# Seven-product Up from the middle of the second chunk on, instead of from the third chunk on

## The chip, the core and the metric

The kernel runs on one core of one Trainium2 chip. The metric is the device time of one execution in microseconds. In the profile the engines are PE (TensorE, the matmul engine; PEld is its weight load), DVE (VectorE), ACT (ScalarE), POOL (GpSimd) and SP (SyncE, which issues most of the DMAs).

## What is computed

An mLSTM cell over 4 batches, 8 heads, 768 steps and a head dimension of 40, followed by a feed-forward block. Cut to what matters, the reference is:

```python
# cell, for every step t:  C and n are the state, m a running maximum
m_new = max(f + m, i);  fs = exp(f + m - m_new);  is_ = exp(i - m_new)
C = fs * C + is_ * outer(v, k);   n = fs * n + is_ * k
y = sigmoid(o) * (C @ q) / max(abs(n @ q), 1)
# feed-forward on x = y, as (3072 tokens, 320)
h = x @ w_in            # 320 -> 2048
g = h * cos(h)
out = g @ w_out         # 2048 -> 320
```

## The kernel before

The sequence is cut into 6 chunks of 128 steps (C = 128, B = 4 batches, NC = 6). A cell is one chunk of one batch: n = chunk * 4 + batch, N = 24. The cell is computed in chunk form: scores (L553), a weighing by decays (`decay_exponents` on POOL, `decay` on ACT, `weigh` on DVE), values (L568) that also read the carried state, and the increment of the state (`seam`, `state`, `fade`).

The feed-forward part of chunk c runs while the cells of chunk c + 1 are computed. It has 16 blocks of 128 hidden units; a **slot** (c, f2), f2 = 0 to 7, takes two of them: Up (x @ w_in for 512 tokens and two blocks), the gate (near, rest, sin, gate), and a share of the down products. A cell takes two slots: slots 2b and 2b + 1 hold cell n = (c + 1) * 4 + b.

The order of work on each engine is the order of the program: everything runs under `tc.manual_schedule()`, so an instruction that waits holds up all that stands behind it on its engine. Between engines there are only the waits that data asks for.

There are two kinds of Up:

- `Up` (L731): per slot four 128x512 matmuls (L749) and two for the last 64 dimensions (L743). It is used in chunks 0 and 1.
- `UpFast` (L806): the same 2x2 block product with seven half-size products (L817, 256 columns) instead of eight. It reads sums of the weights (S1, S2, S4 and, in place of A21, S3, made by `up_weight_sums` on POOL, L779) and sums of x (T1, T2, T4 and one block of x changed in place, made by `x_sums` on POOL, L798 to L804). Its first product is S2 by T2, its second S3 by the changed block of x. After four products ACT copies both banks out (L825, L826), `fill()` puts down products on TensorE in between, three products follow, POOL adds up the copies (L834 to L836), and `join` (L839) adds them on DVE to what stands in PSUM. Gate 0 is then a DVE instruction (L769), gate 1 one of POOL (L852). It is used from chunk `fast` = 2 on.

The two orders of a slot are written out by hand: `both_parts` (for `Up`) and `both_parts_fast` (for `UpFast`), and the main loop chooses between them by chunk. In `both_parts_fast` the scores of a cell are made one slot ahead, so its first slot has an order of its own (`first`).

The down products are taken from a generator, `products_of(c)`: 96 per chunk, 12 for each slot's pair of blocks; `down_slot` (L1068) says how many run in a slot, `fill_in` how many lie between the products of an Up. In chunk 1 seven slots run 12 each, and the last 12 run in slot (2,0) and (2,1). In later chunks slots 2 to 7 run 14 each.

Further names in what follows: `turn_blocks` (L532) transposes q and k of a cell on DVE (L538); `scale_q` (L540) multiplies the turned q by the carried decay on POOL (L542) into qG; `weight_sums(part)` (L883) makes the sums for the down products on POOL, two pairs of blocks per part (L891 to L894); `weigh_k` is L481, `odd_values` L487, `fade` L684, `state` L726; `sums` (L896) is L902 to L905. L1014 is the matmul of a down product. Each float32 matmul shows as two records in the trace.

In `both_parts`, the end of the second slot of a cell is, before the change:

```python
turn_blocks(n + 1)
if n + 1 < (fast + 1) * B:
    scale_q(n + 1)
if b > 0:
    up_weight_sums(b - 1)
if b == B - 1:
    x_sums(c + 1)
```

Of the kernel before, what the change touches and what calls it, by code (L numbers as in the profile page):

```python
# [29 lines left out]
def kernel(  # L30
# [22 lines left out]
    B, H, S, D = q.shape  # L53
# [546 lines left out]
    def normalize_turned(n):  # L600
        denominators(n)
        divide(n)
# [169 lines left out]
    wi = w_in_sb.rearrange("p i (f e n) -> p i f e n", e=2, n=128)  # L772
    A11, A12, A21, A22 = (wi[:, i, :, e] for e in range(2) for i in range(NK))
    HB = B // 2 * C
    fast = 2
    Sw, Tx = {}, {}
    x_room = const.tile([128, 3 * B // 2, C], FP, name="x_room")

    def up_weight_sums(part):  # L779

        tt = nc.gpsimd.tensor_tensor
        S1, S2, S4 = (room[:, i] for i in range(3))
        Sw[0] = S1, S2, S4, A21
        if part == 0:
            tt(out=S1, in0=A21, in1=A22, op=OP.add)
            tt(out=S2, in0=S1, in1=A11, op=OP.subtract)
        elif part == 1:
            tt(out=S4, in0=A12, in1=S2, op=OP.subtract)
        r = ((), range(0, 4), range(4, NF // 2))[part]
        if r:  # L790
            r = slice(r[0], r[-1] + 1)
            tt(out=A21[:, r], in0=A11[:, r], in1=A21[:, r], op=OP.subtract)

    def x_block(c, i, t):
# [259 lines left out]

    def filled(c, f2):

        return c >= fast

    def products_of(c):
        if c not in made_of:  # L1060
# [7 lines left out]
    def down_slot(c, f2):  # L1068

        if c == 0:  # L1070
            if f2 > 0:
                down(0, f2 - 1)
            return
        if f2 == 0:
            if c == 1:
                down(0, LAST)
            else:
                run(made_of[c - 1], 12 - 2 * FILL)
            return
        if f2 == 1 and c > 1:  # L1080
            run(late_products(c - 1), NF)
            return
        each = 14 if c == NC - 1 else 12
        quota = [0] * 8
        for m in range(2, 8):
            quota[m] = each * 7 * (m - 1) // 6 - each * 7 * (m - 2) // 6
        if c == NC - 1:
            quota = [0, 0, 14, 14, 14, 14, 14, 21]
        run(products_of(c), each if c == 1 else quota[f2] - FILL * filled(c, f2))

    pw, pmu = (ps_u.tile([128, HP, C], FP, name=name, tag="up") for name in ("pw", "pmu"))

# [354 lines left out]
    def both_parts(c, b):  # L1447

        n = (c + 1) * B + b
        for i in range(2):  # L1450
            f2 = 2 * b + i
            up = Up(c, f2)
            if i == 0:
                scores(n)
            elif n % 2 == 1 and n + 3 < N:
                load_two(n + 3)
            for e in range(2):
                up.near(e)
            for e in range(2):
                up.rest(e)  # L1460
            if i == 0:
                weigh(n)
                decay_exponents(n + 1)
                for e in range(2):
                    up.sin(e)
                    up.gate(e)
                sums(c, f2)
                if b == B - 1:
                    sigmoid_in_place(c + 2)
                decay(n + 1)  # L1470
            else:
                seam_out(n)
                state(n)
                for e in range(2):
                    up.sin(e)
                    up.gate(e)
                sums(c, f2)
                weigh_k(n + 1)
                odd_values(n + 1)
            down_slot(c, f2)  # L1480
            if i == 0:
                values(n)
                seam(n)
                normalize_turned(n)
                fade(n)
                if b < 3:
                    weight_sums(b + 1)
                load_blocks(n + 2)
                load_E(n + 3)
                if b == B - 2:  # L1490
                    load_o(c + 2)
                sin_next()
            else:
                turn_blocks(n + 1)
                if n + 1 < (fast + 1) * B:
                    scale_q(n + 1)
                if b > 0:
                    up_weight_sums(b - 1)
                if b == B - 1:
                    x_sums(c + 1)  # L1500

    def both_parts_fast(c, b):

        n = (c + 1) * B + b
        cell, follows = n < N, n + 1 < N
        first = (c, b) == (fast, 0)
        ahead = {0: 3, B - 1: 2}.get(b, H - 2)
        pool = nc.gpsimd if cell else nc.vector
        for i in range(2):
            f2 = 2 * b + i  # L1510
            up = UpFast(c, f2, lambda: fill_in(c, f2))
            if f2 == 0:
                if cell:
                    place_gates(c + 1)
                if cell and not first:
                    weigh_k(n)
                sin_next()
            if f2 == 2 * B - 2 and c + 2 < NC:
                sigmoid_in_place(c + 2)
                sin_next()  # L1520
            if cell and i == 0:
                if first:
                    scores(n)
                    scale_q(n)
                else:
                    values(n)
                    seam(n)
                    if f2 > 0 and follows:
                        turn_blocks(n + 1)
                if follows:  # L1530
                    decay_exponents(n + 1)
            if cell and i == 1:
                if follows:
                    decay(n + 1, range(ahead, H))
                    sin_next()
                    if f2 > 1:
                        scores(n + 1)
                if n % 2 == 1 and n + 3 < N:
                    load_two(n + 3)
                if b == B - 1:  # L1540
                    x_sums(c + 1)
                    if follows:
                        scale_q(n + 1)
                elif follows:
                    weigh_k(n + 1)
                    odd_values(n + 1)
                    scale_q(n + 1)
                if b == 0:
                    if first:
                        fade(n)  # L1550
                    sums(c, 0, pool)
            up.join()
            if first and i == 0:
                weigh(n)
            for e in range(2):
                up.near(e)
            for e in range(2):
                up.rest(e)
            if f2 == 2 and cell:
                combine_late(c - 1)  # L1560
            if cell and i == 0 and not first:
                fade(n)
            if cell and i == 1:
                seam_out(n)
            for e in range(2):
                up.sin(e)
                up.gate(e)
            if f2 == 0 and follows:
                turn_blocks(n + 1)
            if f2 == 1 and cell:  # L1570
                state(n)
            if f2 == 0 and not cell:
                sums(c, 0, pool)
            if f2 == 2:
                sums(c, 1, pool)
            down_slot(c, f2)
            if f2 == 1 and follows:
                scores(n + 1)
            if f2 == 0:
                for p in range(2):  # L1580
                    combine_first(c - 1, p)
                for p in range(2):
                    combine_x(c - 1, p)
            if cell and i == 0:
                if follows:
                    decay(n + 1, range(ahead))
                if first:
                    values(n)
                    seam(n)
                normalize_turned(n)  # L1590
                if n + 2 < N:
                    load_blocks(n + 2)
                if n + 3 < N:
                    load_E(n + 3)
                if b == B - 2 and c + 2 < NC:
                    load_o(c + 2)
            if i == 0:
                if f2 > 0:
                    if cell:
                        state(n)  # L1600
                    sums(c, f2)
            if i == 1:
                if follows:
                    if b == B - 1:
                        odd_values(n + 1)
                    weigh(n + 1)
                if b == 0:
                    combine_y(c - 1)
                    if not cell:
                        combine_late(c - 1)  # L1610
                else:
                    sums(c, f2)

    pieces, outs = [], []
    with tc.manual_schedule():
        first_cells()
        first_period()
        for b in range(1, B):
            first_parts(b)
        for c in range(1, NC):  # L1620
            for b in range(B):
                (both_parts_fast if c >= fast else both_parts)(c, b)
        run(made_of[NC - 1], 21)
        combine_last()

# [29 lines left out]
```

## Time and profile before

| | |
|---|---|
| median of 3 runs | 505.82 us (504.16 to 506.86) |
| the profiled execution | 503.72 us, span 501.9 us |
| granted TensorE clock over the span | 1.00 |
| busy: PE, DVE, ACT, POOL | 495.1, 420.6, 332.5, 300.0 us |
| slots (1,4) to (1,7), starts | 154.18, 165.25, 173.11, 184.18 us |
| slots (2,0) to (2,2), starts | 192.04, 202.15, 213.07 us |

Busy times are unions of the instructions of an engine. The starts are those of the first matmul of each Up in the timeline of TensorE; the length of a slot is the distance to the next start. A group in brackets, [5.55 <-DVE t L538], is idle time of that engine ahead of the instruction, and what ended it.

### The profile page before, as it was taken

The numbers are of one execution on the slowest core, as the hardware profiler recorded it, in microseconds if no ns is written. First come the engines' busy times: TensorE is split into PE (matmuls) and PEld (weight loads), VectorE is DVE, ScalarE is ACT, GpSimd is POOL, SyncE is SP. The second block draws the span as 40 slices with busy tenths as digits, with TensorE's granted clock in tenths as the row PEclk, the third lists the DMA queues.
The fourth block names the chain that finished last, engine by engine and source line by source line (L and its number), as shares of the span: only waits on it lengthen the run. The fifth ranks groups of instructions, "written<-read, shape, count | busy, mean of one in ns | idle before, by whom it ended". The sixth has DMA issues, their size and how long they took to land.

```text
span 501.9 us, 11143 instructions
## 1 busy us (share of the span) xinstructions
PE 495.1 (99%) x4038; PEld 375.4 (75%) x4038; DVE 420.6 (84%) x842; ACT 332.5 (66%) x646; POOL 300.0 (60%) x394
## 2 busy tenths in 40 slices
PE   9999999999999999999999999999999999999997
PEld 6856656565667668887887888788788888787876
DVE  7899998999878878899889889889979866777565
ACT  6799997878564575765877846777847743443541
POOL 8254557666555576787558877657567446434340
PEclk9999999999999999999999999999999999999999
DMA  9989899997366346129446118628113000010001
GB/s 139 182 223 239 213 224 279 233 217 136 114 178 111 101 120 127 50 86 202 132 125 106 48 54 195 168 83 150 43 35 85 1 7 5 2 54 0 2 0 54
DMA packets 100663, 56.74 MB, mean 113 GB/s; under 512 B 63456, under 2 KB 93360, under 8 KB 100608
## 3 DMA queue, kind: packets, MB, share of 16 engines
q1 hardware_dynamic: 97408, 54.43, 46.8%
q10 hardware_dynamic: 2896, 1.23, 1.0%
q8 instruction: 32, 0.52, 0.5%
q0 software_dynamic: 304, 0.36, 0.3%
q14 instruction: 23, 0.19, 0.1%
HBM read 50.66 MB, written 4.10 MB: 109 GB/s over the span
## 4 chain that ended last, share of the span: by engine, by line
PE 85%; ACT 4%; DVE 3%; DMA 2%; SPq 2%; POOL 2%; issue 1%; DVEq 0%; ACTq 0%; POOLq 0%
PE acc L1014 24%; PE pup L817 17%; PE pup L749 9%; PE po L863 6%; PE pup L833 6%; PE late L1014 5%; PE ps L560 4%; PE pup L743 3%; PE vt L595 2%; PE vt L586 2%; PE pu L701 2%; PE ph L576 1%; DMA E<-M_d 1%; DMA vs<-in_v_dram 1%; DVE n L760 1%
## 5 line engine op out<-in xcount | busy, mean ns | idle before, releaser
L757 ACT ACTIVATE n<-pup 128x512 int32<-128x512 f32 x64 | 37.0, 593 | 84.2 <-DVE pup L842 58.4
L765 ACT ACTIVATE n<-n 128x512 f32<-128x512 f32 x96 | 57.7, 626 | 16.5 <-DVE n L760 12.5
L852 POOL TENSOR_TENSOR g<-g,n 128x512 f32<-128x512 f32 x31 | 39.6, 1278 | 47.5 <-ACT n L765 47.4
L749 PE MATMUL pup<-xT,w_in_sb 128*128 128x512 f32 x128 | 58.7, 601 | 0.3 <-ACT xT L712 0.2
L1014 PE MATMUL acc<-w_out_sb,g 128*128 128x160 f32 x320 | 58.7, 303 | 0.0
L760 DVE SCALAR_TENSOR_TENSOR n<-pup,n 128x512 f32<-128x512 f32 x64 | 43.1, 689 | 18.5 <-ACT n L757 15.9
L834 POOL TENSOR_TENSOR blocks<-blocks 128x256 f32<-128x256 f32 x32 | 25.1, 785 | 54.5 <-ACT blocks L826 54.5
L1014 PE MATMUL acc<-T,g 128*128 128x160 f32 x304 | 56.4, 301 | 0.0
L817 PE MATMUL pup<-xT,w_in_sb 128*128 128x256 f32 x192 | 53.5, 385 | 0.2
L476 ACT ACTIVATE E<-E,tab 128x128 f32<-128x128 f32 x160 | 50.1, 389 | 4.3 <-POOL E L462 4.1
L1014 PEld LDWEIGHTS acc<-w_out_sb,g 128*128 128x128 f32 x320 | 49.0, 190 | 4.7 <-issue 2.7
L769 DVE TENSOR_TENSOR g<-pup,n 128x512 f32<-128x512 f32 x64 | 42.7, 687 | 5.7 <-ACT n L765 4.8
L1014 PEld LDWEIGHTS acc<-T,g 128*128 128x128 f32 x304 | 46.5, 190 | 1.1 <-issue 0.4
L749 PEld LDWEIGHTS pup<-xT,w_in_sb 128*128 128x128 f32 x128 | 23.1, 189 | 30.7 <-issue 30.0
L825 ACT COPY blocks<-pup 128x512 f32<-128x512 f32 x32 | 18.6, 582 | 34.2 <-PE pup L817 33.8
L817 PEld LDWEIGHTS pup<-xT,w_in_sb 128*128 128x128 f32 x192 | 33.8, 189 | 9.6 <-ACT blocks L826 4.4
L817 PE MATMUL pup<-x_room,room 128*128 128x256 f32 x128 | 38.5, 382 | 0.0
L542 POOL TENSOR_TENSOR qG<-t,G 128x512 f32<-128x512 f32 x20 | 26.4, 1321 | 16.7 <-DVE t L538 16.7
L1014 PE MATMUL acc<-T,blocks 128*128 128x160 f32 x160 | 36.2, 308 | 0.2 <-POOL blocks L904 0.2
L863 PE MATMUL po<-w_out_sb,g 128*128 128x320 f32 x128 | 36.2, 436 | 0.1
L833 PE MATMUL pup<-xL,w_in_l 64*128 64x512 f32 x128 | 36.1, 641 | 0.0
L566 DVE TENSOR_TENSOR E<-ps,E 128x512 f32<-128x512 f32 x46 | 29.5, 682 | 5.8 <-PE ps L560 5.6
(227 smaller groups left out, 1210.7 us busy)
## 6 DMA issues: line engine op xcount, KB each, us to landing
E<-M_d SPq DMA_DIRECT2D x20, 512.0 KB, 6.0
qr<-in_q_dram SPq DMA_DIRECT2D x72, 80.0 KB, 2.6
kr<-in_k_dram SPq DMA_DIRECT2D x72, 80.0 KB, 2.2
bits<-in_moe_w_out_dram SPq DMA_DIRECT2D x8, 640.0 KB, 6.2
G<-G_d SPq DMA_DIRECT2D x18, 256.0 KB, 5.7
blocks<-in_moe_w_in_dram SPq DMA_DIRECT2D x32, 128.0 KB, 4.6
out_dram<-o_sb SPq DMA_DIRECT2D x23, 160.0 KB, 1.8
o<-in_o_gate_dram SPq DMA_DIRECT2D x40, 80.0 KB, 4.4
```

The costliest lines, as they stand in the source:

```text
L476: nc.scalar.activation(out=Es[n][:, h], in_=Es[n][:, h], func=AF.Exp, scale=-1.0, bias=tab[:, c, 0, g:g + 1])
L566: nc.vector.tensor_tensor(out=w, in0=pss[n][j], in1=w, op=OP.mult)
L749: nc.tensor.matmul(pu.rearrange("p (b t) -> p b t", b=B), w_in_sb[:, i, ts(2 * f2 + e, 128)], xT[c][:, i:NK * B:NK], start=(i == 0 and not ...
L757: nc.scalar.activation(out=self.n[e], in_=self.pu[e], func=AF.Copy, bias=0.25)
L760: nc.vector.scalar_tensor_tensor(out=self.n[e].bitcast(FP), in0=self.pu[e], scalar=0.25, in1=self.n[e], op0=OP.add, op1=OP.subtract)
L765: nc.scalar.activation(out=r, in_=r, func=AF.Sin, scale=TWO_PI_DOWN)
L769: nc.vector.tensor_tensor(out=g, in0=self.pu[e], in1=self.n[e].bitcast(FP), op=OP.mult)
L817: nc.tensor.matmul(bank[:, part].rearrange("p (b t) -> p b t", b=B // 2), w[:, f2], x, start=start, stop=stop, skip_group_check=True)
L833: nc.tensor.matmul(pu, w_in_l[r, f2], xL[c][r].rearrange("p b t -> p (b t)"), start=False, stop=True, skip_group_check=True)
L852: tt(out=self.g, in0=self.g, in1=self.n[e].bitcast(FP), op=OP.mult)
L863: nc.tensor.matmul(po[c][b], gs[c, f][:, ts(b, C)], w_out_sb[:, f], start=(f == 0), stop=(f == NF - 1))
L1014: nc.tensor.matmul(a, lhs, rhs, start=start, stop=stop)
```

## The change

The condition `c >= fast` becomes `(c, f2 // 2) >= (1, 2)`: the slots (1,4) to (1,7) use `UpFast` and the order of `both_parts_fast`. With it:

- `up_weight_sums` has four parts now: part 0 (S1, S2) in slot (1,1), part 1 (S4) in (1,2), parts 2 and 3 (the two halves of S3) in (1,3). Before, they were in (1,3), (1,5) and (1,7).
- `x_sums(1)` is added, in (1,3), behind `scale_q(10)`; the guard on `scale_q` in `both_parts` is gone. `x_sums(2)` moves to the place that it has in `both_parts_fast`.
- The first slot in the fast order is (1,4), with cell 10: `scale_q` is no longer in it, `fade` and `weight_sums(3)` follow its values, and it turns the blocks of cell 11 behind its gates.
- Slot (1,3) runs 10 down products instead of 12; (1,4) to (1,7) run 10 and two more in the Up; (2,0) runs 10 and two more.
- `load_o` and `sigmoid_in_place` in `both_parts` go, since `both_parts_fast` has them for the slots in question.

```diff
--- before.py
+++ after.py
@@ -772,7 +772,7 @@
     wi = w_in_sb.rearrange("p i (f e n) -> p i f e n", e=2, n=128)
     A11, A12, A21, A22 = (wi[:, i, :, e] for e in range(2) for i in range(NK))
     HB = B // 2 * C
-    fast = 2
+    FAST = 1, B // 2
     Sw, Tx = {}, {}
     x_room = const.tile([128, 3 * B // 2, C], FP, name="x_room")
 
@@ -786,9 +786,8 @@
             tt(out=S2, in0=S1, in1=A11, op=OP.subtract)
         elif part == 1:
             tt(out=S4, in0=A12, in1=S2, op=OP.subtract)
-        r = ((), range(0, 4), range(4, NF // 2))[part]
-        if r:
-            r = slice(r[0], r[-1] + 1)
+        else:
+            r = (slice(4, NF // 2), slice(0, 4))[part - 2]
             tt(out=A21[:, r], in0=A11[:, r], in1=A21[:, r], op=OP.subtract)
 
     def x_block(c, i, t):
@@ -1054,7 +1053,7 @@
 
     def filled(c, f2):
 
-        return c >= fast
+        return (c, f2 // 2) >= FAST
 
     def products_of(c):
         if c not in made_of:
@@ -1075,7 +1074,7 @@
             if c == 1:
                 down(0, LAST)
             else:
-                run(made_of[c - 1], 12 - 2 * FILL)
+                run(made_of[c - 1], 12 - FILL if c == 2 else 12 - 2 * FILL)
             return
         if f2 == 1 and c > 1:
             run(late_products(c - 1), NF)
@@ -1086,7 +1085,7 @@
             quota[m] = each * 7 * (m - 1) // 6 - each * 7 * (m - 2) // 6
         if c == NC - 1:
             quota = [0, 0, 14, 14, 14, 14, 14, 21]
-        run(products_of(c), each if c == 1 else quota[f2] - FILL * filled(c, f2))
+        run(products_of(c), (each - FILL * (f2 > 2)) if c == 1 else quota[f2] - FILL)
 
     pw, pmu = (ps_u.tile([128, HP, C], FP, name=name, tag="up") for name in ("pw", "pmu"))
 
@@ -1461,12 +1460,12 @@
             if i == 0:
                 weigh(n)
                 decay_exponents(n + 1)
+                if b == 1:
+                    up_weight_sums(1)
                 for e in range(2):
                     up.sin(e)
                     up.gate(e)
                 sums(c, f2)
-                if b == B - 1:
-                    sigmoid_in_place(c + 2)
                 decay(n + 1)
             else:
                 seam_out(n)
@@ -1483,27 +1482,26 @@
                 seam(n)
                 normalize_turned(n)
                 fade(n)
-                if b < 3:
-                    weight_sums(b + 1)
+                weight_sums(b + 1)
                 load_blocks(n + 2)
                 load_E(n + 3)
-                if b == B - 2:
-                    load_o(c + 2)
                 sin_next()
             else:
                 turn_blocks(n + 1)
-                if n + 1 < (fast + 1) * B:
-                    scale_q(n + 1)
-                if b > 0:
-                    up_weight_sums(b - 1)
-                if b == B - 1:
-                    x_sums(c + 1)
+                if b == 0:
+                    up_weight_sums(0)
+                else:
+                    up_weight_sums(2)
+                scale_q(n + 1)
+                if b == 1:
+                    x_sums(c)
+                    up_weight_sums(3)
 
     def both_parts_fast(c, b):
 
         n = (c + 1) * B + b
         cell, follows = n < N, n + 1 < N
-        first = (c, b) == (fast, 0)
+        first = (c, b) == FAST
         ahead = {0: 3, B - 1: 2}.get(b, H - 2)
         pool = nc.gpsimd if cell else nc.vector
         for i in range(2):
@@ -1512,7 +1510,7 @@
             if f2 == 0:
                 if cell:
                     place_gates(c + 1)
-                if cell and not first:
+                if cell:
                     weigh_k(n)
                 sin_next()
             if f2 == 2 * B - 2 and c + 2 < NC:
@@ -1521,7 +1519,6 @@
             if cell and i == 0:
                 if first:
                     scores(n)
-                    scale_q(n)
                 else:
                     values(n)
                     seam(n)
@@ -1546,8 +1543,6 @@
                     odd_values(n + 1)
                     scale_q(n + 1)
                 if b == 0:
-                    if first:
-                        fade(n)
                     sums(c, 0, pool)
             up.join()
             if first and i == 0:
@@ -1565,13 +1560,13 @@
             for e in range(2):
                 up.sin(e)
                 up.gate(e)
-            if f2 == 0 and follows:
+            if (f2 == 0 or first and i == 0) and follows:
                 turn_blocks(n + 1)
             if f2 == 1 and cell:
                 state(n)
             if f2 == 0 and not cell:
                 sums(c, 0, pool)
-            if f2 == 2:
+            if f2 == 2 and c > 1:
                 sums(c, 1, pool)
             down_slot(c, f2)
             if f2 == 1 and follows:
@@ -1587,7 +1582,10 @@
                 if first:
                     values(n)
                     seam(n)
+                    fade(n)
                 normalize_turned(n)
+                if first:
+                    weight_sums(3)
                 if n + 2 < N:
                     load_blocks(n + 2)
                 if n + 3 < N:
@@ -1619,7 +1617,7 @@
             first_parts(b)
         for c in range(1, NC):
             for b in range(B):
-                (both_parts_fast if c >= fast else both_parts)(c, b)
+                (both_parts_fast if (c, b) >= FAST else both_parts)(c, b)
         run(made_of[NC - 1], 21)
         combine_last()
```

## The prediction

> **What bounds the kernel now.** First the page: its busy times, then the chain of work that ended last.
>
> ```profile
> span 501.9 us, 11143 instructions
> PE 495.1 (99%) x4038; PEld 375.4 (75%) x4038; DVE 420.6 (84%) x842; ACT 332.5 (66%) x646; POOL 300.0 (60%) x394
> ...
> PE 85%; ACT 4%; DVE 3%; DMA 2%; SPq 2%; POOL 2%; issue 1%; DVEq 0%; ACTq 0%; POOLq 0%
> ```
>
> TensorE is the bound: it is never idle for as much as a microsecond between 40 and 437 us, so a microsecond of matmul saved is a microsecond of the kernel, and a microsecond that TensorE waits is one lost for good. Second, the timeline of TensorE, where a slot is the time from the first matmul of one Up to that of the next. Slot (1,3), the last before the change's first seven-product slot, reads:
>
> ```profile
> 146.32 1.13 PE L743 MATMUL pup<-xL,w_in_l 64*128 64x512 f32 x4
> 147.38 3.70 PE L749 MATMUL pup<-xT,w_in_sb 128*128 128x512 f32 x8
> ...
> 153.91 0.43 PE L1014 MATMUL acc<-w_out_sb,blocks 128*128 128x160 f32 x2
> 154.18 3.60 PE L749 MATMUL pup<-xT,w_in_sb 128*128 128x512 f32 x8
> ```
>
> It is 7.86 us long, and slot (1,4) begins at 154.18 with no gap. Third, POOL and VectorE in the same stretch (start, us, line; the bracket is idle time and what ended it):
>
> ```profile
> 150.00 0.86 POOL L894 TENSOR_TENSOR T<-w_out_sb,T 128x320 f32<-128x320 f32 x1
> ...
> 151.49 0.30 POOL L487 COPY vr<-vs 128x128 f32<-128x128 f32 x1
> 157.35 1.27 POOL L542 TENSOR_TENSOR qG<-t,G 128x512 f32<-128x512 f32 x1 [5.55 <-DVE t L538]
> 158.58 2.36 POOL L785 TENSOR_TENSOR room<-w_in_sb 128x1024 f32<-128x1024 f32 x1
> ```
>
> ```profile
> 150.95 1.49 DVE L760 SCALAR_TENSOR_TENSOR n<-pup,n 128x512 f32<-128x512 f32 x2 [1.68 <-ACT n L757]
> 152.36 0.87 DVE L726 TENSOR_TENSOR st<-st,pu 40x128 f32<-40x128 f32 x4
> 153.25 1.29 DVE L769 TENSOR_TENSOR g<-pup,n 128x512 f32<-128x512 f32 x2
> ...
> 155.83 0.42 DVE L905 TENSOR_TENSOR blocks<-g,blocks 128x256 f32<-128x256 f32 x1
> 156.18 1.09 DVE L538 STREAM_TRANSPOSE t<-qr 128x512 f32<-128x512 f32 x1
> ```
>
> The reader is to see that scale_q(10), L542, stands still on POOL for 5.55 us until VectorE has transposed q, and that this transpose comes at the end of a chain that hangs on slot (1,3)'s own Up: rest, state, gates, sums, turn. It ends at 157.26, 3.1 us after TensorE has already begun the next slot. Today this costs nothing, as what is queued behind L542 isn't wanted soon. The order on each engine is the program's.
>
> **The gain: four slots by seven products.** I take each slot's dense length from the slot of today that it will resemble; slot starts are read from the TensorE timeline. One down product is two records, 0.136 us apart (32 late records take 4.37 us), so 0.27 us. Today (1,3) to (2,1) are 7.86, 11.07, 7.86, 11.07, 7.86, 10.12, 10.92: 66.76 us. After:
> - (1,3): two products fewer, 7.86 - 0.54 = 7.32.
> - (1,4): the order of today's first fast slot (2,0), 10.12, with two products more: 10.66.
> - (1,5) and (1,7): (2,5) is 9.00 with 14 products; 12 here: 8.46 each. (1,6): (2,4), 10.24 - 0.54 = 9.70.
> - (2,0): (3,0), 9.55, plus the two products left over: 10.09. (2,1): (3,1), 10.60.
>
> Together 65.29, **1.47 us less**. It is small since seven 256-wide products and their copies replace four 512-wide ones on an engine that was dense either way.
>
> **The first price: x_sums behind scale_q.** Today's own first fast slot has these rows on POOL ahead of it:
>
> ```profile
> 187.31 1.26 POOL L792 TENSOR_TENSOR w_in_sb<-w_in_sb 128x512 f32<-128x512 f32 x1 [1.29 <-PE pup L749]
> 188.53 0.73 POOL L801 TENSOR_TENSOR x_room<-xT 128x256 f32<-128x256 f32 x1
> ...
> 190.83 0.73 POOL L804 TENSOR_TENSOR xT<-xT 128x256 f32<-128x256 f32 x1
> ```
>
> The guard skips scale_q(12) there, so the four x_sums run at once and are over at 191.56, just before TensorE asks at 192.04. The change drops the guard and puts x_sums(1) behind scale_q(10) on POOL. UpFast(1,4) stands first on TensorE in its slot: its first product reads T2 (second sum), its second reads what the fourth writes in xT (L804). Scores, values and every down product of the slot are queued behind it. So: the half of A21 (1.26) fits in POOL's idle 151.8 to 157.3; scale_q(10) still ends at 158.62; the sums, 0.8 apart, end T2 at 160.15 and L804 at 161.6. The first product (0.43) runs at 160.25, the rest from 161.75, as if the slot began at 161.3. Dense, TensorE would be there at 146.32 + 7.32 = 153.64. **Price 7.7 us.** Nothing ahead of the transpose gets shorter: its chain begins at Up(1,3)'s end, 151.0, which doesn't move.
>
> **The second price: the clock.** Such an idle stretch occurs nowhere inside the kernel today, but at its ends:
>
> ```profile
> L1096 PE MATMUL pw<-room x10: 379/634/634, 1.0 to 9.2; 128*128 128x512 bf16 x10
> ```
>
> ```profile
> 501.00:503.00 2.00, 0.00 (x0) 0.00 (x0) 0.00 (x0) 0.00 (x0) 0.00 (x0) 0.88 0.00 0
> ```
>
> The opening matmuls, after idleness, take 634 ns where the same form later takes 379, and follow each other at 0.427 instead of 0.216 us for 3.2 us. The last matmul ends at 498.36; the granted clock of 0.88 over 501 to 503 is half speed from 502.5 on, 4.1 us after. TensorE's idle stretch here is 6.3 us up to the lone first product, so I take a drop to half and one opening ramp: 3.2 us at half speed, **1.6 us**. Bounds: 0, if the drop doesn't come, to 3.2 for a ramp of twice the length. [...]
>
> **The third price: weight_sums(3) in the first fast slot.** It moves behind fade(10) there. In (2,0) today U, the end of Up, is 196.82, and gate 1 on POOL (L852) ends at 202.40, U + 5.6. Values end near U + 5.5 with two more products, fade takes 1.8 (164.62 to 166.44), weight_sums four times 0.93: POOL is free at U + 11.2. Slot (1,5) begins at U + 5.85, so its three adds (L834 to L836) begin 5.35 us into it; in (2,5) they begin at 2.64. The second ends at about 7.0, the third at 7.8. VectorE's join, near, rest, sin and gate 0 then end at about 10.8 (in (2,5) gate 0 ends 8.6 into the slot). TensorE wants that bank 0.86 us after the next slot's start, at 8.46 + 0.86 = 9.32. **Price 1.5 us**; bounds 0, if POOL's chain is a little shorter than each step here, and 2.2, the whole lateness of the join. VectorE's lateness then is gone by (1,7): even slots leave it over a microsecond.
>
> **Costs taken at nothing.** S1 and S2 (2.36 and 2.37) move to (1,1), where POOL stands idle 5.8 us ahead of scale_q(9). S4 (2.37) goes before fade(9), which waits 4.2 us for values now. Uncovered they would cost 2.4 each. They slow VectorE beside them: its 0.42 us sum took 1.19 at 163.73, beside POOL's 1.30 us select. The 1.3 to 1.7 us gaps ahead of VectorE's rest take that up. weigh_k(12), 0.72, goes with (2,0), as in (3,0). DMA issues keep their slots.
>
> **Sum.** -1.5 + 7.7 + 1.6 + 1.5 = +9.3 us. The profiled execution is 503.72 us, 1.8 of it around the span: 513.0. The median of runs is 2.1 above it, 505.82, so the forecast for a median is **515.1 us**.
>
> **Rivals.**
> - *Only the first wait.* The clock holds through an idle stretch broken by one product, and POOL gets through (1,5) in time: 505.82 - 1.5 + 7.7 = 512.0. For it: the lone product, and a third price worked out from six steps of tenths. Against: the 4.1 us. Chance 0.28.
> - *The seven products arrive on time.* At the one place (1,3)/(1,4), POOL reaches x_sums by about 151 us, so that L804 is over by 154. It decides there: q would have to be turned 6 us before the 157.26 of today, hence ahead of the gates of its own slot, or x_sums not wait in order. Then the gain stands alone, 504.3. The program's order on VectorE and POOL, as the timelines show it, speaks against. Chance 0.10.
> - *Forecast.* 0.62.
>
> **How the numbers follow.** About 0.5%, 2.5 us, is what a measurement of this kernel can tell from no change; the three runs alone span 2.7. Both cases with the first wait lie over 1% above the median: slower 0.90. The on-time case is -0.3%: 0.07 same, 0.03 faster, for the spread. The range goes from 512.0 less the runs' 1.7 to the forecast plus 1.6 (clock), 0.7 (third price) and 1.0 (runs): 510.3 to 518.4.
>
> **What would show it.** In the profile after: POOL's first L801 directly behind an L542 that ended its wait on L538; TensorE idle some 6 us before the first L817 and released by POOL L802 or L804; a granted clock under 1 right after, with L817 matmuls of over 600 ns; L834 in (1,5) behind L894, over 5 us into the slot; slots (1,5) to (1,7) near 8.5, 9.7, 8.5 otherwise. It is wrong if the first L817 follows the last L1014 of (1,3) within a microsecond.

## The result and the profile after

The changed kernel takes 518.09 us (median of 4 runs, 517.63 to 520.18) against 505.19 us for the kernel before on the same chip: a ratio of 1.0268, 95% interval 1.0239 to 1.0297. That is 12.9 us slower. The forecast was 9.3 us slower; carried by the ratio, 505.82 us would have become 519.4, above the range's 518.4. The direction and the first cause were right. What was missing is worked out below.

The profiled execution of the changed kernel took 518.46 us. The page, with the chain that ended last:

```profile
span 516.5 us, 11242 instructions
PE 499.2 (97%) x4062; PEld 381.5 (74%) x4062; DVE 426.7 (83%) x846; ACT 338.7 (66%) x656; POOL 318.7 (62%) x414
...
PE 60%; DVE 10%; ACT 6%; DMA 5%; SPq 4%; POOL 3%; issue 3%; ACTq 0%; DVEq 0%; POOLq 0%
```

TensorE is still busy 97% of the time, but its share of the chain has fallen from 85% to 60%: the chain now goes through waits, and behind them through VectorE and the transfers. (Line numbers from L792 on are one lower than before.) Who TensorE waited for, in us in total, times, and the longest:

```profile
PE pup L816 <- POOL x_room L801: 6.3, 1, 6.3
PE pup L816 <- DVE g L769: 2.0, 2, 1.3
PE ps L560 <- DVE t L538: 1.0, 1, 1.0
```

The first line is the wait that was forecast. POOL and TensorE around it, from the timelines:

```profile
153.81 1.28 POOL L791 TENSOR_TENSOR w_in_sb<-w_in_sb 128x512 f32<-128x512 f32 x1
159.44 1.28 POOL L542 TENSOR_TENSOR qG<-t,G 128x512 f32<-128x512 f32 x1 [4.35 <-DVE t L538]
160.68 0.72 POOL L800 TENSOR_TENSOR x_room<-xT 128x256 f32<-128x256 f32 x1
...
162.97 0.73 POOL L803 TENSOR_TENSOR xT<-xT 128x256 f32<-128x256 f32 x1
```

```profile
155.48 0.43 PE L1013 MATMUL acc<-T,g 128*128 128x160 f32 x2
162.26 1.22 PE L816 MATMUL pup<-x_room,room 128*128 128x256 f32 x2 [6.35 <-POOL x_room L801]
163.75 2.07 PE L816 MATMUL pup<-xT,w_in_sb 128*128 128x256 f32 x4 [0.27 <-POOL xT L803]
```

scale_q(10) waits for the turned q, the sums of x stand behind it, and TensorE's first two products are released by L801 and L803, one after the other. The clock over the stretch (window, length, busy time and count of each engine, then the granted clock, DMA share and GB/s):

```profile
155.90:158.60 2.70, 0.01 (x1) 0.00 (x0) 2.60 (x7) 0.00 (x0) 0.00 (x0) 1.00 0.87 125
158.60:162.30 3.70, 0.04 (x1) 0.04 (x1) 1.68 (x2) 0.00 (x0) 2.70 (x4) 0.50 0.34 88
162.30:168.80 6.50, 6.23 (x15) 4.72 (x16) 0.00 (x0) 1.17 (x2) 3.96 (x5) 0.50 0.21 53
168.90:176.60 7.70, 7.70 (x117) 6.32 (x115) 5.66 (x9) 4.11 (x7) 3.36 (x4) 1.00 0.00 0
```

The granted clock halves 2.7 us into the idle stretch and stays at half for 6.6 us behind it, from the first product at 162.26 on. Slot lengths in us, read as before from the starts of the Ups, against the forecast's own steps (its prices put where it put them):

| slots | before | forecast | after |
|---|---|---|---|
| (1,2) | 11.07 | 11.07 | 12.38 |
| (1,3) and (1,4) | 18.93 | 27.28 | 28.15 |
| (1,5) and (1,6) | 18.93 | 19.66 | 20.40 |
| (1,7) | 7.86 | 8.46 | 8.45 |
| (2,0) | 10.12 | 10.09 | 10.73 |
| (2,1) | 10.92 | 10.60 | 10.84 |
| together | 77.83 | 87.16 | 90.95 |

The slots of this table hold 13.1 of the 14.6 us by which the spans of the two profiled executions differ (the medians differ by 12.9). Of the rest, 0.6 us lie in slot (0,3), which the change doesn't touch.

### The profile page after: what moved, and what is told of

It is laid out like the page before. It is cut to its first block, busy times and chain, and to the rows that moved or that the text cites. A ratio compares the mean times of both kernels' runs of the same rounds, so it can differ in the third digit from the quotient of the medians.

```text
span 516.5 us, 11242 instructions
## 1 busy us (share of the span) xinstructions
PE 499.2 (97%) x4062; PEld 381.5 (74%) x4062; DVE 426.7 (83%) x846; ACT 338.7 (66%) x656; POOL 318.7 (62%) x414
## 4 chain that ended last, share of the span: by engine, by line
PE 60%; DVE 10%; ACT 6%; DMA 5%; SPq 4%; POOL 3%; issue 3%; ACTq 0%; DVEq 0%; POOLq 0%
PE acc L1013 21%; PE pup L816 20%; PE pup L832 7%; PE late L1013 4%; PE ps L560 3%; DMA blocks<-in_moe_w_in_dram 2%; DMA vs<-in_v_dram 2%; DVE n L760 2%; PE vt L595 2%; DVE t L538 2%; DMA qr<-in_q_dram 1%; PE vt L586 1%; ACT n L765 1%; ACT n L757 1%; ACT E L476 1%
## 5 line engine op out<-in xcount | busy, mean ns | idle before, releaser
L851 POOL TENSOR_TENSOR g<-g,n 128x512 f32<-128x512 f32 x35 | 44.7, 1278 | 53.4 <-ACT n L765 53.2
L833 POOL TENSOR_TENSOR blocks<-blocks 128x256 f32<-128x256 f32 x36 | 29.0, 806 | 58.3 <-ACT blocks L825 58.3
L816 PE MATMUL pup<-xT,w_in_sb 128*128 128x256 f32 x216 | 62.1, 393 | 2.6 <-DVE g L769 2.0
L760 DVE SCALAR_TENSOR_TENSOR n<-pup,n 128x512 f32<-128x512 f32 x60 | 40.5, 689 | 12.7 <-ACT n L757 10.3
L816 PE MATMUL pup<-x_room,room 128*128 128x256 f32 x144 | 44.3, 390 | 6.3 <-POOL x_room L801 6.3
L824 ACT COPY blocks<-pup 128x512 f32<-128x512 f32 x36 | 20.9, 580 | 40.9 <-PE pup L816 39.2
L769 DVE TENSOR_TENSOR g<-pup,n 128x512 f32<-128x512 f32 x60 | 40.4, 688 | 7.5 <-ACT n L765 6.6
L749 PE MATMUL pup<-xT,w_in_sb 128*128 128x512 f32 x96 | 44.1, 602 | 0.8 <-DVE g L769 0.6
L841 DVE TENSOR_TENSOR pup<-pup,blocks 128x256 f32<-128x256 f32 x36 | 15.7, 437 | 35.3 <-PE pup L832 33.5
L832 PE MATMUL pup<-xL,w_in_l 64*128 64x512 f32 x144 | 40.6, 641 | 0.0
L1013 PE MATMUL acc<-w_out_sb,blocks 128*128 128x160 f32 x160 | 34.1, 303 | 0.0
```

Source lines behind the costliest of these rows:

```text
L749: nc.tensor.matmul(pu.rearrange("p (b t) -> p b t", b=B), w_in_sb[:, i, ts(2 * f2 + e, 128)], xT[c][:, i:NK * B:NK], start=(i == 0 and not ...
L760: nc.vector.scalar_tensor_tensor(out=self.n[e].bitcast(FP), in0=self.pu[e], scalar=0.25, in1=self.n[e], op0=OP.add, op1=OP.subtract)
L769: nc.vector.tensor_tensor(out=g, in0=self.pu[e], in1=self.n[e].bitcast(FP), op=OP.mult)
L816: nc.tensor.matmul(bank[:, part].rearrange("p (b t) -> p b t", b=B // 2), w[:, f2], x, start=start, stop=stop, skip_group_check=True)
L832: nc.tensor.matmul(pu, w_in_l[r, f2], xL[c][r].rearrange("p b t -> p (b t)"), start=False, stop=True, skip_group_check=True)
L833: nc.gpsimd.tensor_tensor(out=s[:, 1], in0=s[:, 1], in1=s[:, 0], op=OP.add)
```

## The experiments

In all of them "dense" means the slot lengths of the forecast without its three prices: 54.7 us from the start of (1,3) to that of (2,1), where the kernel before needs 55.8.

**The order on POOL.** x_sums(1) goes ahead of scale_q(10):

```diff
-                scale_q(n + 1)
                 if b == 1:
                     x_sums(c)
+                scale_q(n + 1)
+                if b == 1:
                     up_weight_sums(3)
```

> The changed kernel with x_sums(1) ahead of scale_q(10) on POOL, all else as changed. Theory (the wait of the first seven-product slot is POOL's order): POOL is free at 155.1, T2 is made by 156.7 and the fourth sum by 158.2, so TensorE waits about 2 us instead of 7.7, too short for the clock to fall, and the 3.3 us of half speed go as well: 518.1 - 5.5 - 3.3 = about 509.3. Rival 1 (the slow matmuls after the wait have another cause than the wait): about 512.6. Rival 2 (the sums themselves, or the transpose on VectorE, hold the slot, not the place of scale_q): 517 to 518.

It took 511.84 us, 1.0136 times the kernel before (1.0107 to 1.0164): 6.2 us less than the changed kernel, not 8.8. The waits of TensorE:

```profile
PE pup L816 <- ACT blocks L824: 1.4, 2, 1.3
...
PE pup L816 <- POOL xT L803: 1.0, 1, 1.0
PE pup L816 <- POOL x_room L801: 0.7, 1, 0.7
```

The two waits for the sums are 1.7 us together where 2 were expected, and the granted clock stays at 1.0: slots (1,3) and (1,4) take 20.44 us instead of 28.15. The place of scale_q is the cause, and the second rival falls. But scale_q(10) and the half of S3 behind it now stand in front of POOL's adds of (1,4). VectorE's join waits 3.13 us for them, ACT is late with all that follows, and its copy L824 makes TensorE wait 1.3 us in (1,5), which takes 10.92 us instead of 9.18. The wait removed came back in part as another one.

**The clock by itself.** 24 matmuls that nobody reads run inside the wait:

```diff
+            if (c, f2) == (1, B):
+                some = ident.bitcast(BF)[:, 0:128]
+                for _ in range(24):
+                    nc.tensor.matmul(b0.rearrange("p (h t) -> p h t", h=HP), some, some.unsqueeze(1).to_broadcast([128, HP, 128]), start=True, stop=True)
             product(b1, second, S2, T2, True, True)
```

> The changed kernel with 24 matmuls of 128x512 in bf16 that nobody reads, ahead of the first product of slot (1,4), in a bank that this product's group starts afresh: 5.2 us of work inside the wait. Theory (idleness halves the clock): the wait for POOL's L801 stays where it is, the granted clock stays at 1.0, the products behind take 379 ns, and 3.3 us go: about 514.8. Rival (the first products are slow because of their operands or of POOL beside them): 518.1, products of 600 ns and over all the same.

It took 516.06 us (1.0233, 1.0192 to 1.0273), 2.0 us less than the changed kernel for more work. The intervals of the two ratios overlap, so it is the trace that decides. TensorE's timeline and the clock of the slot:

```profile
155.33 5.35 PE L822 MATMUL pup<-ident 128*128 128x512 bf16 x24 [0.20 <-DVE g L769]
161.48 0.70 PE L816 MATMUL pup<-x_room,room 128*128 128x256 f32 x2 [0.80 <-POOL x_room L801]
```

```profile
161.50:167.90 6.40, 5.62 (x34) 4.10 (x36) 0.34 (x2) 1.17 (x2) 5.14 (x7) 1.00 0.19 52
```

The first product starts 13.83 us into (1,3), as in the changed kernel (13.82), and the clock is 1.00. Slot (1,4) falls from 14.33 to 11.82: half speed cost 2.5 us there. It isn't 3.3 mostly because the wait for the fourth sum, 0.27 us at half speed, is 0.79 at full speed.

**S1 and S2 elsewhere.** Two placements, one after the other. First into (0,7), where POOL stands idle:

```diff
                 on_vector(made[1:2])
+                if b == B - 1:
+                    up_weight_sums(0)
...
-                if b == 0:
-                    up_weight_sums(0)
-                else:
+                if b == 1:
                     up_weight_sums(2)
```

> The changed kernel with S1 and S2 made in slot (0,7), where POOL stands idle 7.15 us, instead of in (1,1). Theory (S2 on POOL stretched VectorE's sum in (1,1) from 0.42 to 2.05 us, and with it the turn of k that the scores of (1,2) wait for): that wait of 1.0 us goes, slot (1,2) is 11.07 again, 1.3 us less: about 516.8. Rival (the scores wait for something else, or VectorE is held as long in (0,7)): 518.1.

It took 522.11 us (1.0335, 1.0306 to 1.0365), 3 to 4 us more than the changed kernel. Slot (1,2) is 11.07 again, as the theory has it, but (0,7) is 3.15 and (1,0) 1.67 us longer. POOL and VectorE in (0,7):

```profile
109.53 2.35 POOL L785 TENSOR_TENSOR room<-w_in_sb 128x1024 f32<-128x1024 f32 x1
```

```profile
110.11 1.80 DVE L616 SCALAR_TENSOR_TENSOR d<-dt,least 128x8 f32<-128x8 f32 x1
```

An instruction on 8 columns that takes 0.17 to 0.26 us in the kernel before and in the changed one takes 1.80, and ends as POOL's S1 ends. In (0,7) VectorE is on the path, and its hold-ups reach TensorE, which waits twice, 1.5 us each time. The 1.67 us of (1,0) are the clock's. Behind the two waits it was at half for 3.4 us:

```profile
119.10:122.50 3.40, 3.40 (x6) 1.44 (x5) 3.27 (x8) 3.37 (x6) 0.71 (x1) 0.50 1.08 139
```

Idle time on POOL is not free room. Then S2 alone, out of (1,1) and in front of S4:

```diff
             tt(out=S1, in0=A21, in1=A22, op=OP.add)
-            tt(out=S2, in0=S1, in1=A11, op=OP.subtract)
         elif part == 1:
+            tt(out=S2, in0=S1, in1=A11, op=OP.subtract)
             tt(out=S4, in0=A12, in1=S2, op=OP.subtract)
```

> The changed kernel with S1 alone in (1,1) and S2 in front of S4 in (1,2). Theory (it is S2's run beside VectorE's sum of (1,1), not POOL's total, that makes the scores of (1,2) wait): the sum L901 takes 0.42 us again, slot (1,2) is 11.07 instead of 12.38 in the trace, and the sums of (1,2), which nobody waits for at once, are stretched instead. Rival (POOL's chain, through scale_q(9) or the decays, holds (1,2)): 12.4 or more, since POOL now has 4.7 us there.

A single execution: 516.49 us. What it tells is in the trace. In the changed kernel S2 on POOL and the first of VectorE's sums were

```profile
135.87 2.35 POOL L786 TENSOR_TENSOR room<-room,w_in_sb 128x1024 f32<-128x1024 f32 x1
```

```profile
136.46 2.05 DVE L901 TENSOR_TENSOR blocks<-g 128x256 f32<-128x256 f32 x1
```

and here that sum is

```profile
135.65 0.43 DVE L901 TENSOR_TENSOR blocks<-g 128x256 f32<-128x256 f32 x1
```

Slot (1,2) is 11.07 us, the 1.0 us wait of the scores is gone, and 4.7 us of sums on POOL within (1,2) itself cost nothing. So it is one overlap, not POOL's total, that made (1,2) longer.

**weight_sums(3) out of the way.** It moves ahead of gate 1 in (1,4):

```diff
                 if follows:
                     decay_exponents(n + 1)
+                if first:
+                    weight_sums(3)
...
-                if first:
-                    weight_sums(3)
```

> The changed kernel with weight_sums(3) in POOL's 4.26 us of idleness ahead of gate 1 of slot (1,4) instead of behind fade(10). Theory (there it held back POOL's three adds of (1,5), so join and gate 0 came late): the adds begin 2.6 us into (1,5) instead of 4.8, the waits of 0.35 and 1.26 us for VectorE at (1,5) and (1,6) go, 1.6 us less: about 516.5. Rival (VectorE's own work is what makes the gate late there): the waits stay, 518.

It took 517.04 us (1.0266, 1.0239 to 1.0292), by the ratio the same as the changed kernel. In its trace (1,4) is 1.1 us shorter, as the stretch at half speed was shorter, 6.8 us against 10.2. Slots (1,5) and (1,6) take 20.57 us, against 20.40. POOL's adds were on time, and the gate was late all the same. POOL's second add, then VectorE's last sum and the join, then the wait:

```profile
178.09 0.72 POOL L834 TENSOR_TENSOR blocks<-blocks 128x256 f32<-128x256 f32 x1
```

```profile
180.98 1.38 DVE L904 TENSOR_TENSOR blocks<-g,blocks 128x256 f32<-128x256 f32 x1
182.38 0.43 DVE L841 TENSOR_TENSOR pup<-pup,blocks 128x256 f32<-128x256 f32 x1
```

```profile
PE pup L816 <- DVE g L769: 2.2, 2, 1.5
```

The second add ends at 178.81, and the join, which needs it, begins at 182.38, right behind VectorE's sums. The rival holds: the join waits for VectorE's own row of work, not for POOL's adds. It did so in the changed kernel too, where POOL's second add ended at 183.15, VectorE's last sum at 184.30, and the join began at 184.33. The theory's mechanism of the third price falls.

**Everything moved.** Five kernels keep seven products from (1,4) on and place POOL's work by the traces. The first puts S1 and S2 in (0,7), S4 and half of S3 in (1,1), all sums of x but the last in (1,2), scale_q(10) behind the first Up, weight_sums(3) in (1,5) and (1,6):

> Seven products from the same slot on, with POOL's work placed by the trace: S1 and S2 in (0,7); S4 and one half of S3 in (1,1); T1, T2 and T4 in (1,2); only the change of x in place in (1,3); scale_q(10) behind the first Up in (1,4); weight_sums(3) in two halves in (1,5) and (1,6), the other half of S3 in (1,5). Theory (every loss of the changed kernel is a place on POOL): the dense gain alone is left, 505.2 - 1.5 = about 503.7, with no wait of TensorE over 0.5 us. Rival (POOL's sums hold VectorE wherever they lie, and a slot with 12 products is too short for the gate): 505 to 507, with waits for L769 at the starts of (1,6) or (2,0).

514.82 us (1.0191, 1.0162 to 1.0221): over the theory's 503.7, and over the rival's 505 to 507 as well. The long wait is gone, but (0,7) is 3.2 us longer as above, and (1,3) to (2,0) take 60.3 us instead of 54.7. The second, the halves kernel, makes only the halves of the weight sums that slots 4 to 7 need:

```diff
-    def up_weight_sums(part):
+    def up_weight_sums(part, r):
...
-                scale_q(n + 1)
-                if b == 1:
-                    x_sums(c)
-                    up_weight_sums(3)
+                if b == 0:
+                    up_weight_sums(0, 1)
+                    up_weight_sums(1, 1)
+                    scale_q(n + 1)
+                else:
+                    x_sums(c, (3, 2))
```

> Seven products from the same slot on, only the halves of S1, S2, S4 and S3 for slots 4 to 7 made before (1,4), in (1,1) and (1,2) and clear of VectorE's sum; T1, T2 in (1,2), the change of x and T4 in (1,3); scale_q(10) behind the first Up; weight_sums(3) ahead of gate 1 in (1,4); the other halves one by one in (1,5), (1,6), (1,7). Theory (all losses are POOL's places): slots (1,1) to (2,1) within 1 us of the dense lengths, 504.5 - 1.5 = about 503.0. Rival (the fast order in slots of 12 products is bound by VectorE whatever POOL does): (1,5) to (2,0) stay 2 to 3 us over the dense lengths, about 505.5.

512.76 us (1.0178, 1.0161 to 1.0194). (1,1) to (1,4) are 7.86, 11.07, 7.77 and 10.74: dense, or within 0.5 us of it, so the first wait and the loss in (1,2) are both removable. But the late half of S3 stood behind the sums of x on POOL and made (2,0) wait:

```profile
PE pup L810 <- POOL w_in_sb L785: 3.0, 1, 3.0
```

```profile
194.10:197.00 2.90, 0.61 (x4) 0.21 (x2) 2.50 (x5) 1.48 (x3) 2.90 (x3) 1.00 0.37 104
197.10:203.80 6.70, 6.11 (x16) 4.95 (x16) 2.14 (x5) 2.61 (x6) 4.27 (x7) 0.50 0.00 0
```

Slot (2,0) took 15.94 us, 5.9 over the dense 10.09: 3.0 for the wait, and the rest mostly for the clock, which was at half for 6.8 us. The third kernel spreads POOL's work again (weight_sums(2) into (1,4), the late half of S3 into (1,6)), the fourth takes kw and qG of (1,5) from beside VectorE's sums:

> Seven products from the same slot on, with POOL's work placed once more: S1 in (1,1); S2 and S4 in (1,2); in (1,3) the half of S3 for slots 4 to 7 and all sums of x, as weight_sums(2) goes to (1,4), ahead of gate 1; scale_q(10) behind the first Up; weight_sums(3) in two halves in (1,6) and (1,7), the other half of S3 in (1,6), well before (2,0) asks for it. Theory (the 5.8 us of (2,0) in b2_halves were that half of S3 on POOL and the halved clock; what stays is VectorE's lateness in (1,5) and (1,6), some 2 us over the dense lengths, as its sums run beside POOL's adds, kw and qG): -1.5 + 2 to 3 us against before, about 505. Rival (the losses follow POOL's total, not its places): 508 or more, with a new wait of over 2 us for POOL.

```diff
-                elif follows:
+                elif follows and not first:
                     weigh_k(n + 1)
...
+            if first and i == 1:
+                weigh_k(n + 1)
+                odd_values(n + 1)
+                scale_q(n + 1)
```

> b3_spread with weigh_k(11) and scale_q(11) of slot (1,5) behind gate 1 on POOL. Theory (VectorE's four sums of slot (1,4), 0.42 us each alone, are stretched to over 3 us by POOL's kw and qG beside them, and the join of (1,5) stands behind them): the sums take 2.4 us or less, the wait at (1,6) for L769 falls from 1.5 by about 0.8 us: 0.8 us below b3_spread. Rival (VectorE's count of instructions in (1,4) and (1,5) is too long even unstretched): the wait at (1,6) stays within 0.3 us.

They took 511.98 (1.0156, 1.0124 to 1.0188) and 512.33 us (1.0153, 1.0117 to 1.0188): no difference in time. The trace has one. VectorE's last sum of slot (1,4), in the third and then in the fourth:

```profile
171.76 1.38 DVE L897 TENSOR_TENSOR blocks<-g,blocks 128x256 f32<-128x256 f32 x1
```

```profile
172.88 0.43 DVE L897 TENSOR_TENSOR blocks<-g,blocks 128x256 f32<-128x256 f32 x1
```

The four sums take 2.3 us instead of 3.8, the wait at (1,6) falls from 1.51 to 0.82, and (1,5) and (1,6) together from 20.88 to 19.39, where dense is 18.16. So the stretching by kw and qG is 1.5 of the 2.7 us by which the two slots were late. In (1,7) the fourth kernel gave it back, 10.66 against 8.80: kw and qG now ran beside VectorE's next four sums, which took 4.1 us instead of 2.1. In both, (2,0) still takes 15.2 us, with waits of 1.2 us for the sums of x and 2.1 for kw(12), and the clock at half for 3.4 us behind the second. That is what the third kernel's rival had named, 508 us or more and a new wait of over 2 us for POOL. The last run moves that half of S3 into POOL's idle time in (1,3):

> b4_k_behind with the half of S3 for slots 0 to 3 made in POOL's idle time of (1,3) instead of in (1,6). Theory (in b4_k_behind POOL's adds of (1,7), the sums of x for (2,0) and kw(12) stand behind that half and weight_sums, which cost (1,7) 2.2 and (2,0) some 4.5 us): (1,7) near 8.5, the wait of (2,0) for the sums of x gone, that for kw(12) under 1 us, (1,5) and (1,6) as in b4_k_behind: about 5 us below it, 505 to 507. Rival (the losses of (1,7) and (2,0) follow VectorE's lateness, not POOL's): less than 2 us below it.

512.32 us (1.0145, 1.0112 to 1.0178). Against the fourth, (2,0) falls from 15.18 to 12.66 and (1,7) from 10.66 to 10.14, 3.0 of the 5 us expected. Of these an estimated 1.7 are the clock, which stays at 1.0 in (2,0) (half of the 3.4 us at half speed that the fourth kernel has there). The wait for the sums of x is gone, that for kw(12) is still 1.5 us, and (1,7) did not come near 8.5. The medians do not show this, as its runs scatter from 510.1 to 514.8, and its profiled execution lost 3 us before slot (0,0). From (1,3) to (2,1) it still takes 60.7 us against 55.8 before. No kernel here beats the one before.

## Why the forecast was right in kind and too low

**The gain** was not seen. Two dense lengths hold: (1,7) is 8.45 against the forecast's 8.46, and in the later kernels (1,4) is 10.74 against 10.66. But (1,3) never fell below 7.77, against 7.32: with the sums in time, the first product of (1,4) still waits 0.29 us for gate 0 of (1,3) (the halves kernel). The shortest length that any run had for each slot from (1,3) to (2,1) adds up to 67.8 us, 1.0 more than the 66.76 of the kernel before.

**The first price** was right in cause, place and size. With the clock kept up (the 24 idle matmuls), (1,3) and (1,4) take 13.83 + 11.82 = 25.65 us; the forecast without its clock term was 7.32 + 7.7 + 10.66 = 25.68.

**The second price** was too small: 1.6 taken, 2.5 measured in the slot, inside its bounds of 0 to 3.2. The step that failed is the ramp: I took the 3.2 us of the kernel's start, but half speed lasted 6.6 us of work here, and 4.4, 5.6 and 5.2 in the three other runs with the same wait. The rival in which the clock holds through the wait falls. The half-speed stretch here is 10.2 us long, from 158.6 to 168.9; the ones with weight_sums(3) moved and of the halves kernel are 6.8. What set these lengths was not shown.

**The costs taken at nothing** are the step that failed outright: 1.3 us in (1,2). I had seen POOL's work stretch a sum of VectorE's from 0.42 to 1.19 us, and named VectorE's gap ahead of rest as the cover. But the scores of (1,2) stand right behind its Up and wait for the turn of k. The turn and the scores, before and then after:

```profile
138.20 1.08 DVE L538 STREAM_TRANSPOSE t<-kr 128x512 f32<-128x512 f32 x1
139.74 1.06 PE L560 MATMUL ps<-t,t 40*128 40x128 f32 x16
```

```profile
140.62 1.07 DVE L538 STREAM_TRANSPOSE t<-kr 128x512 f32<-128x512 f32 x1
141.75 1.16 PE L560 MATMUL ps<-t,t 40*128 40x128 f32 x16 [1.04 <-DVE t L538]
```

Before, the turn ended at 139.28 and the scores began some 0.5 us later: 0.5 to 0.6 us of cover for a delay of 1.6. I asked what VectorE would do next, and not who waits for its transpose. The 2.05 us sum began 0.6 us after S2 and ended 0.3 us after it.

**The third price** had about the right size at its place (waits of 0.35 and 1.26 us in two slots that are 2.2 us over dense, 1.5 forecast) and the wrong mechanism, so the size is luck. weight_sums(3) can go and the wait stays: VectorE is late in the first fast slot, where it has to turn, normalize, add to the state and make its sums between two joins, and what POOL does beside them (the adds, kw, qG) stretches those sums from 1.7 us (four of 0.42) to 3.4. My claim that the lateness is gone by (1,7) was wrong as well. (1,7) itself is dense, but (2,0) waits 0.76 us for gate 0, and (1,5), (1,6), (2,0) and (2,1) are together 1.6 us over the forecast.

Together: 1.3 (S2 beside the sum), 0.9 (clock) and 1.6 (VectorE behind the first slot) are the 3.8 us between 87.16 and 90.95.

**The rival of the other sign**, sums in time, falls at the place that was named: L803 ended at 163.7, not by 154.

What stays open is whether some other placement would leave a gain. The five tried leave at least 5.6 us more than dense from (1,3) to (2,0). They suggest a reason and don't prove it: behind the first fast slot VectorE works without a gap up to its join, so what POOL does beside its sums there can make the join later.

## What to carry to other kernels

When a step joins an in-order queue, ask first what stands ahead of it there and what that waits for: a guard that looks like bookkeeping (scale_q skipped for one cell) kept a whole wait off the path. For work moved into another engine's idle time, look up which instructions of other engines it stretches, and who is waiting for those: here VectorE's 0.42 us sum took 2.05 beside POOL's S2, and the scores waited 1.0 us. And price a long wait of the matmul engine at more than its own length, because the clock can fall with it: here an estimated 1.7 us (half of 3.4 at half speed) on top of a wait of 2.1, about 2.9 on top of 3.0 and 2.5 on top of 6.3.

## What the runs showed of the hardware that was not expected

- Behind a wait of TensorE of 2.1 us the granted clock was at half for 3.4 us (third and fourth kernel of "Everything moved", (2,0)), and behind one of 3.0 us for 6.8 (the halves kernel). Waits of 0.7 and 1.0 us, with one product between, left it at 1.0 (x_sums(1) ahead of scale_q(10)). After the same 6.3 us wait the half-speed work lasted 6.6, 4.4, 5.6 and 5.2 us in four runs.
- Behind two waits of 1.5 us in (0,7), with S1 and S2 moved there, it was at half for 3.4 us, from 119.1 to 122.5.
- VectorE's hold-up was not in proportion to its instruction's own size: one on 8 columns, of 0.17 to 0.26 us elsewhere, took 1.80 beside POOL's 2.35 us sum, and one of 0.42 us took 2.05 beside another of 2.35.
- Three of VectorE's 0.42 us sums in a row, beside POOL instructions of 0.90, 0.90 and 1.45 us, took 0.83, 0.94 and 1.38 us, each ending 0.3 us after POOL's (weight_sums(3) moved, (1,5)).
